# Holding half of the second pass's late weights in a pair of group buffers, with a closer pace for conv backward and parameter chunks

## The chip, the cores and the metric

The kernel runs on one core of one Trainium2 chip. The metric is the device time of one execution in microseconds (us). The core has five engines with a queue each: TensorE (PE, matrix products, with its weight loads listed as PEld), VectorE (DVE), ScalarE (ACT), GpSimd (POOL) and SyncE (SP), and 16 DMA engines, which all queues share. Each engine works through its own instructions in the order fixed when the kernel is compiled; an instruction that waits holds up those behind it.

## The reference

Forward and backward of one block on 2048 tokens of width D = 576: a layer norm, a state-space convolution (S4) with N = 128 states per channel, and a gated feed-forward layer with F = 4608 hidden units.

```
xn = layernorm(x)
s  = conv(xn, K) + xn * Dskip,   K = Re sum_n C exp(dt A l) dt B   (by FFT, length 2 L)
h  = silu(xn @ w1) * (xn @ w3)
g  = silu(h @ w2)
out = x + s * g
return out, and gradients by x, A_re, A_im, B_re, B_im, C_re, C_im, log_dt, Dskip, w1, w3, w2
```

The part that matters here is the gradient by x through the feed-forward layer: with GG and GU the gradients at the two hidden products (2048 x 4608 each), it is GG @ w1^T + GU @ w3^T, added to the gradient from the convolution and taken through the layer norm.

## The kernel before

Tokens are cut into 16 row tiles of 128 (LT), the hidden width into 36 f tiles of 128 (FT) or 18 groups of 256 (FG, NG). A framework places tiles in memory, makes all waits and orders the instructions of each engine by a priority in planned microseconds, which the code sets with `at(us)`; instructions of different parts are so woven into each other. A planned unit takes more than one real microsecond: the backward part starts at unit 700, which is 850 us in the trace, and the second pass at unit 1348, which is 1700 us.

The backward part (L1125) lays these strands beside each other:

- 18 groups, one each 36 units (L1157 to L1161). A group loads its transposed w2 slice (SP) and the stored forward values G and U (POOL) into one of two sets of three buffers, `gg_n`, `h_n` and `gu_n`, 8 KB per partition each. Even groups use the set `e_in0`, odd groups `e_in1` (L1139, L1188). It computes GG and GU in place, stores them to DRAM (L1236), and forms the gradients of w2 (L1251), w3 and w1 (L1270, L1276, L1278). The last even group is 16, the last of all is 17.
- The conv backward (L876) in four quarters of D, `TQ` = 75 units each: transforms on TensorE, complex products on VectorE, copies on ScalarE.
- The parameter chunks (L902): 36 chunks of 16 channels, one each `TC` = 14 units from the end of conv on. Each is loaded two chunks ahead (`gz`, `pz`, and `qT` by a transposing DMA, L1007 to L1012), takes 16 small products (L1025), then 8 products and 4 reduces on VectorE (L1032, L1036). After them comes `phase5_final` (L1040), the gradients of the state-space parameters.
- The second pass (`phase6_inputs`, L1285) from unit T2 = T0 + 36 * 18 = 1348 on: for each row tile it loads GG and GU transposed (`ggc`, `guc`, L1300, 36 f tiles each, in `x_in`, two sets) and multiplies them with the transposed weights (L1312), 144 products per row tile, one row tile each `TX` = 18 units. Then `finish` adds the conv gradient and does the layer norm's backward.

The transposed weights (L1166) are cut by f tiles into parts. Part 0 (f tiles 0 to 15) is in `x_wA` and loaded 150 units before T2. Parts 1 and 2 (16 to 25, 26 to 35) are in `x_wB`, in memory that the groups' buffers free. Each part is 5 transposing DMAs per matrix: four of 128 rows of D and one of 64. The first two row tiles (`head` = 2) are worked part by part, so that products can start before all weights are there; their loads are issued by parts too (L1329 to L1334). Row tile 2 takes the buffers of row tile 0 when that one is done. All transposing DMAs go through SP's queue, mixed with chunk loads and stores of outputs.

The memory of the two stacks is taken in the order in which the pools are opened: on the left `persist`, then `go_keep` (the kept output gradient, 37 KB), then `e_w`, `e_in0`, `e_in1`; when the groups end, `x_in` and `x_wB` take that space from the bottom.

Of the kernel before, what the change touches and what calls it, by code (L numbers as in the profile page):

```python
# [14 lines left out]
BF16 = mybir.dt.bfloat16  # L15
I32 = mybir.dt.int32
P = 128
# [43 lines left out]
class K:  # L61
# [1063 lines left out]
    def backward(self, T0, TG, TQ, TC, TX, gctx, mats):  # L1125
        nc, cfg = self.nc, self.cfg
        D, L, LT, F, FT = cfg.D, cfg.L, cfg.LT, cfg.F, cfg.FT
        self.GG_dram = self.dram.tile([LT, P, F], BF16, name="GG_dram")
        self.GU_dram = self.dram.tile([LT, P, F], BF16, name="GU_dram")
        self.GXN_dram = self.dram.tile([P, LT, D], FP32, name="GXN_dram")  # L1130
        NG = F // self.FG
        T2 = T0 + TG * NG
        FA = 16
        pool = self.tc.tile_pool
        PS = bass.MemoryType.PSUM
        with ExitStack() as out:
            ffn = ExitStack()
            wp = ffn.enter_context(pool(name="e_w", bufs=2))
            inp = [ffn.enter_context(pool(name=f"e_in{k}", bufs=1)) for k in range(2)]  # L1139
            elp = ffn.enter_context(pool(name="e_el", bufs=3))  # L1140
            gwp = ffn.enter_context(pool(name="e_gw", bufs=2))
            ps_h = ffn.enter_context(pool(name="e_ps_h", bufs=3, space=PS))
            ps_gw = ffn.enter_context(pool(name="e_ps_gw", bufs=2, space=PS))
            ps = out.enter_context(pool(name="b_ps", bufs=3, space=PS, side="right"))
            self.ssm_bwd_conv(T0, TQ, ps)
            mats.close()
            fix = out.enter_context(pool(name="b_fix", bufs=1, side="right"))
            S_all = fix.tile([P, 4, D], FP32, name="S_all")
            wA = out.enter_context(pool(name="x_wA", bufs=1, side="right"))
            self.at(T2 - 150)  # L1150
            wT = [self.load_wT(wA, 0, FA)]
            T1 = T0 + 4 * TQ
            self.ssm_bwd_params(T1, TC, S_all, ps)
            self.at(T1 + TC * D // 16)
            self.phase5_final(out, fix, S_all, ps, T1 + TC * D // 16, TX)
            cur = self.phase6_load(0, T0 - TG, TG, wp, inp)
            for gi in range(NG):  # L1157
                nxt = self.phase6_load(gi + 1, T0 + TG * gi, TG, wp, inp) if gi + 1 < NG else None
                self.at(T0 + TG * gi)
                self.phase6_group(gi, cur, elp, gwp, ps_h, ps_gw)  # L1160
                cur = nxt  # L1161
            ffn.close()
            gctx.close()
            self.phase6_inputs(T2, TX, FA, wT)

    def load_wT(self, pool, f0, f1):  # L1166
        cfg = self.cfg
        tiles = []
        for w in ("B_w1", "B_w3"):
            t = pool.tile([P, f1 - f0, cfg.D], BF16, name=f"wT{w}{f0}")  # L1170
            for (do, dsz) in cfg.dch:
                self.nat_transpose(t[:, :, do:do + dsz], self.aps[w][do:do + dsz, f0 * P:f1 * P])
            tiles.append(t)
        return tiles

    def nat_transpose(self, dst, src):
        self.nc.sync.dma_start_transpose(out=dst, in_=src)  # L1177
# [107 lines left out]
    def phase6_inputs(self, T2, TX, FA, wT):  # L1285
        nc, cfg = self.nc, self.cfg
        D, DT, L, LT, F, FT = cfg.D, cfg.DT, cfg.L, cfg.LT, cfg.F, cfg.FT
        aps = self.aps
        pieces = self.dpieces()
        with self.tc.tile_pool(name="x_in", bufs=2) as inp, \  # L1290
                self.tc.tile_pool(name="x_wB", bufs=1) as wB, \
                self.tc.tile_pool(name="l_sb", bufs=2) as sb, self.tc.tile_pool(name="l_sm", bufs=4) as sm, \
                self.tc.tile_pool(name="x_ps", bufs=2, space=bass.MemoryType.PSUM) as ps:
            FM = (FA + FT) // 2
            parts = [(0, FA), (FA, FM), (FM, FT)]
            head = 2

            def load(tiles, i, f0, f1):
                for t, src in zip(tiles, (self.GG_dram, self.GU_dram)):
                    self.nat_transpose(t[:, f0:f1, :], src[i][:, f0 * P:f1 * P])  # L1300

            def alloc(i):
                acts = [inp.tile([P, FT, P], BF16, name=n) for n in ("ggc", "guc")]
                px = [ps.tile([P, 512], FP32, name=f"px{pi_}") for pi_ in range(len(pieces))]
                return acts, px

            def products(acts, px, p):
                f0, f1 = parts[p]
                for fi in range(f0, f1):
                    for ai, act in enumerate(acts):  # L1310
                        for pi_, (po, pw) in enumerate(pieces):
                            nc.tensor.matmul(px[pi_][:, 0:pw], lhsT=act[:, fi, :], rhs=wT[p][ai][:, fi - f0, po:po + pw],  # L1312
                                             start=(fi == 0 and ai == 0), stop=(fi == FT - 1 and ai == 1))

            def finish(i, px):
                gx = sb.tile([P, D], FP32, name="gx7")
                gxs = sb.tile([P, D], FP32, name="gxs7")
                nc.scalar.dma_start(out=gxs[:], in_=self.GXN_dram[:, i, :])
                go_t = sb.tile([P, D], BF16, name="go7")
                nc.scalar.dma_start(out=go_t[:], in_=aps["grad_out"].flatten_outer_dims()[i * P:(i + 1) * P, :])  # L1320
                for pi_, (po, pw) in enumerate(pieces):
                    nc.vector.tensor_tensor(out=gx[:, po:po + pw].rearrange("p (g d) -> p g d", g=4),  # L1322
                                            in0=px[pi_][:, 0:pw].rearrange("p (g d) -> p g d", g=4),
                                            in1=self.perm(gxs[:])[:, :, pi_, :], op=ALU.add)
                self.ln_bwd_tile(sb, sm, gx, i, go_t)

            self.at(T2)
            first = [alloc(i) for i in range(head)]
            for i in range(head):  # L1329
                load(first[i][0], i, *parts[0])  # L1330
            for p in (1, 2):
                wT = wT + [self.load_wT(wB, *parts[p])]
                for i in range(head):
                    load(first[i][0], i, *parts[p])  # L1334
            for p in range(3):
                for i in range(head):
                    self.at(T2 + TX * (head * parts[p][0] + i) / FT)
                    products(*first[i], p)
            for i in range(head):
                finish(i, first[i][1])  # L1340
            for i in range(head, LT):
                self.at(T2 + TX * i)
                acts, px = alloc(i)
                load(acts, i, 0, FT)
                for p in range(3):
                    products(acts, px, p)
                finish(i, px)

# [30 lines left out]
def kernel(  # L1379
# [34 lines left out]
    k = K(tc, aps, {})  # L1414
    with k.ctx:
# [4 lines left out]
        mats = ExitStack()  # L1420
# [3 lines left out]
        with tc.tile_pool(name="xT", bufs=1) as xp, tc.tile_pool(name="kg_sel", bufs=1) as selp:  # L1424
            k.prologue(matp, selp, xp)
            with tc.tile_pool(name="f_w", bufs=2) as wp, \
# [5 lines left out]
                k.ffn_output_open(octx, 345)  # L1432
                k.ffn_hidden(wp, gup, fps, 0, 12)
        k.parp_ctx.close()
        gctx = ExitStack()
        gop = gctx.enter_context(tc.tile_pool(name="go_keep", bufs=1))
        k.go_o = gop.tile([P, k.cfg.LT, k.cfg.D], BF16, name="go_o")
# [1 line left out]
        k.goTt = gop.tile([P, k.cfg.L // 2], BF16, name="goTt")  # L1439
        k.ffn_output(480, 10)  # L1440
        octx.close()
        k.backward(700, 36, 75, 14, 18, gctx, mats)


# [28 lines left out]
```

## Time and profile before

| | |
|---|---|
| median of 7 runs | 2079.49 us (2045.48 to 2086.46) |
| profiled execution: its time, its span | 2084.68 us, 2082.9 us |
| granted TensorE clock, mean | 0.943 |
| PE, DVE, ACT, POOL busy | 86%, 72%, 47%, 22% of the span |
| DMA, mean rate | 202 GB/s |
| second-pass products (L1312) | 2304, 488.2 us busy, 60.8 us idle ahead of them |
| parameter products and reduces (L1032, L1036) | 288 of 683 ns, 144 of 1215 ns |
| chain that ended last: second-pass products | 9.4% of the span |

A row of busy time names the engine, the operation and what is written from what; busy time on PE overlaps itself, since products are pipelined: one of 293 ns follows another of its kind after some 122 ns (142 of them took 17.6 us in the chain of waits). Idle time of an engine counts only where it lies on the path that ends last. The last product of the groups ends at 1700.7 us, the last product of all at 2075.9 us.

### The profile page before, as it was taken

Reading aid. Unit: us, or ns where it says so; the run is one execution under the profiler, and the core shown is the slowest. Engines: PE = TensorE matmul, PEld = TensorE weight load, DVE = VectorE, ACT = ScalarE, POOL = GpSimd, SP = SyncE. Lnnn points to the kernel's source line nnn. Section 1 sums busy time; section 2 is a strip of 40 time slices with the busy share of each in tenths; the row PEclk is TensorE's granted clock in tenths of the full one; section 3 lists DMA queues with packets and bytes.
Section 4 is the critical chain, followed back from the end, with each engine's and each line's share of the span. In section 5 each row is a group of like instructions: output and inputs, shape, how many; then the busy total and the mean of one; then the engine's idle time right before and its main releaser. Section 6 shows DMA issues by size and latency. Waiting matters only on the chain. (4 is left out here: it accounts for less than half of the span.)

```text
span 2082.9 us, 40279 instructions
## 1 busy us (share of the span) xinstructions
PE 1798.8 (86%) x16144; PEld 1251.9 (60%) x16214; DVE 1505.9 (72%) x2616; ACT 971.6 (47%) x1735; POOL 460.8 (22%) x610
## 2 busy tenths in 40 slices
PE   2888988889898899989999999977996994699997
PEld 1443333335453577777777777756685772577785
DVE  7459999998684465477787877775995883586862
ACT  1968888886455411574747465433543410000000
POOL 6015556562122111111111211211121210000000
PEclk9899999999999999999999999988998996799998
DMA  6688778777578887546464645999698799999794
GB/s 180 237 277 284 263 263 280 269 266 259 169 269 186 226 206 183 174 132 190 134 187 137 203 122 149 265 213 196 184 204 178 190 188 191 217 229 176 169 182 63
DMA packets 550380, 421.27 MB, mean 202 GB/s; under 512 B 413872, under 2 KB 480624, under 8 KB 545584
## 3 DMA queue, kind: packets, MB, share of 16 engines
q1 hardware_dynamic: 487648, 254.56, 50.9%
q0 software_dynamic: 37904, 147.48, 22.1%
q10 hardware_dynamic: 24640, 16.65, 3.1%
q8 instruction: 127, 2.08, 0.4%
q14 instruction: 61, 0.50, 0.1%
HBM read 135.96 MB, written 196.27 MB: 159 GB/s over the span
## 5 line engine op out<-in xcount | busy, mean ns | idle before, releaser
L1312 PE MATMUL px<-wTB_w,guc 128*128 128x288 bf16 x1152 | 243.6, 293 | 31.9 <-DMA guc<-GU_dram 21.3
L1312 PE MATMUL px<-wTB_w,ggc 128*128 128x288 bf16 x1152 | 244.6, 293 | 28.9 <-DMA wTB_w<-in_B_w_dram 16.1
L1270 PEld LDWEIGHTS <-xn_bf 128*128 128x128 bf16 x2304 | 224.3, 98 | 29.3 <-issue 2.6
L1032 DVE TENSOR_TENSOR pr_q<-et_ps,pz 128x512 f32<-128x512 f32 x288 | 185.9, 683 | 59.2 <-PE et_ps L1025 52.0
L768 PEld LDWEIGHTS <-xnT 128*128 128x128 bf16 x1152 | 102.8, 99 | 175.6 <-issue 81.6
L1224 PE MATMUL ph<-w2T,goT 128*128 128x256 bf16 x1152 | 180.2, 288 | 2.0 <-DVE e L840 2.0
L1036 DVE TENSOR_REDUCE S_all<-pr_q 128x16 f32<-128x1024 f32 x144 | 174.9, 1215 | 2.3
L1251 PE MATMUL pgw<-go_o,h_n 128*128 128x288 bf16 x1152 | 163.5, 291 | 0.0
L768 PE MATMUL pg<-wmB_w,xnT 128*128 128x512 bf16 x523 | 151.1, 394 | 9.1 <-issue 5.6
L768 PE MATMUL pu<-wmB_w,xnT 128*128 128x512 bf16 x565 | 153.5, 388 | 5.0 <-ACT u_t L778 3.9
L1312 PEld LDWEIGHTS <-guc 128*128 128x128 bf16 x1152 | 114.4, 100 | 65.0 <-DMA guc<-GU_dram 23.4
L1312 PEld LDWEIGHTS <-ggc 128*128 128x128 bf16 x1152 | 114.8, 100 | 60.0 <-issue 14.1
L1358 ACT ACTIVATE t<-gx 128x576 f32<-128x576 f32 x16 | 10.9, 684 | 296.4 <-DVE gx L1322 296.4
L1272 ACT CAST gw<-pgw 128x256 bf16<-128x256 f32 x144 | 54.6, 380 | 196.7 <-PE pgw L1270 195.1
L831 PE MATMUL po<-w2g,hc 128*128 128x288 bf16 x1152 | 145.1, 288 | 1.3 <-ACT u_t L778 1.3
L499 POOL COPY pz_k<-p_k 128x256 bf16<-128x256 bf16 x144 | 132.3, 962 | 47.4 <-issue 38.2
L1270 PE MATMUL pgw<-gu_n,xn_bf 128*128 128x256 bf16 x1152 | 132.8, 272 | 1.5 <-ACT gw L1255 1.1
L1230 DVE TENSOR_TENSOR gu_n<-gh,gu_n 128x1024 bf16<-128x1024 bf16 x72 | 49.4, 686 | 117.1 <-ACT gh L1227 117.1
L831 PEld LDWEIGHTS <-hc 128*128 128x128 bf16 x1152 | 112.1, 98 | 31.2 <-issue 1.7
L1224 PEld LDWEIGHTS <-goT 128*128 128x128 bf16 x1152 | 103.7, 102 | 43.9 <-issue 12.8
L1270 PE MATMUL pgw<-gg_n,xn_bf 128*128 128x256 bf16 x1152 | 129.4, 273 | 0.0
L1251 PEld LDWEIGHTS <-h_n 128*128 128x128 bf16 x1152 | 112.3, 100 | 28.3 <-issue 0.7
(315 smaller groups left out, 3921.0 us busy)
## 6 DMA issues: line engine op xcount, KB each, us to landing
G_dram<-g_t POOLq DMA_DIRECT2D x72, 256.0 KB, 4.0
U_dram<-u_t POOLq DMA_DIRECT2D x72, 256.0 KB, 3.7
H_dram<-h_t SPq DMA_DIRECT2D x72, 256.0 KB, 3.3
Q_dram<-q_k SPq DMA_DIRECT2D x36, 512.0 KB, 4.2
gg_n<-G_dram POOLq DMA_DIRECT2D x18, 1024.0 KB, 5.7
h_n<-U_dram POOLq DMA_DIRECT2D x18, 1024.0 KB, 9.3
GU_dram<-gu_n POOLq DMA_DIRECT2D x36, 512.0 KB, 6.2
GG_dram<-gg_n POOLq DMA_DIRECT2D x36, 512.0 KB, 8.8
```

The costliest lines, as they stand in the source:

```text
L499: nc.gpsimd.tensor_copy(out=pz[:, g, h, 1:3], in_=pv[:, g, h])
L768: nc.tensor.matmul(pt[:], lhsT=xnT[:, c, ts], rhs=wm[w][:, c, :], start=(c == 0 and not first), stop=(c == nfull - 1 and first))
L831: nc.tensor.matmul(po_[:, pi_, 0:pw], lhsT=hc[:, fi, :], rhs=w2[fi][:, po:po + pw], start=(fi == 0), stop=(fi == FT - 1))
L1032: nc.vector.tensor_tensor(out=pr[:, r].rearrange("p k m a -> p m k a"), in0=T[h][:, r][:, None].to_broadcast([P, 2, 4, 2, AV]), in1=pz[:, ...
L1036: nc.vector.tensor_reduce(out=S_all[:, :, d0:d0 + 4].rearrange("p (s k) d -> p k s d", k=2), in_=pr[:].rearrange("p r k (s d) a -> p k s d ...
L1224: nc.tensor.matmul(ph[j][:, k, :], lhsT=lw, rhs=rh, start=(n == 0), stop=(n == nfull))
L1230: nc.vector.tensor_tensor(out=pair(t_)[:, :, sl], in0=gh[:], in1=pair(t_)[:, :, sl], op=ALU.mult)
L1251: nc.tensor.matmul(pgw[pi_][:, 0:pw], lhsT=hn[:, tt, fl * P:(fl + 1) * P], rhs=go_o[:, tt, po:po + pw], start=(tt == 0), stop=(tt == LT - 1))
L1270: nc.tensor.matmul(pw_[:, 0:FG], lhsT=self.xn_bf[:, tt, c * P:(c + 1) * P], rhs=nat[:, tt, :], start=(tt == 0), stop=(tt == LT - 1))
L1272: nc.scalar.copy(out=gw[:, c, :], in_=pw_[:, 0:FG])
L1312: nc.tensor.matmul(px[pi_][:, 0:pw], lhsT=act[:, fi, :], rhs=wT[p][ai][:, fi - f0, po:po + pw], start=(fi == 0 and ai == 0), stop=(fi == F ...
L1358: nc.scalar.activation(out=t[:], in_=g, func=ACT.Copy, scale=-invD, accum_out=mg[:])
```

## The change

Four things are edited. The pool `e_in0` is opened before `go_keep` and stays open to the end, so that its three buffers can be used in the second pass. The f tiles 16 to 35 are cut in three parts instead of two, of 7, 7 and 6 f tiles (NH = 16 * 256 // 576 = 7 is what fits in one buffer): w1 and w3 of the first of them and w1 of the second are put into the three buffers of `e_in0`, with a priority of T2 - 40, ahead of the last group; w3 of the second and both of the third go to `x_wB`, which is smaller by that. The first two row tiles are allocated and loaded with priority T2 - 15 instead of T2, in four parts. And TQ goes from 75 to 65, TC from 14 to 13, so that conv ends at unit 960 instead of 1000 and the chunks at 1428 instead of 1504.

```diff
-            inp = [ffn.enter_context(pool(name=f"e_in{k}", bufs=1)) for k in range(2)]
+            inp = [self.in0, ffn.enter_context(pool(name="e_in1", bufs=1))]
...
     def load_wT(self, pool, f0, f1):
         cfg = self.cfg
-        tiles = []
-        for w in ("B_w1", "B_w3"):
-            t = pool.tile([P, f1 - f0, cfg.D], BF16, name=f"wT{w}{f0}")
-            for (do, dsz) in cfg.dch:
-                self.nat_transpose(t[:, :, do:do + dsz], self.aps[w][do:do + dsz, f0 * P:f1 * P])
-            tiles.append(t)
-        return tiles
+        return [self.load_wT1(pool.tile([P, f1 - f0, cfg.D], BF16, name=f"wT{k}_{f0}"), k, f0, f1) for k in range(2)]
+
+    def load_wT1(self, t, k, f0, f1):
+        for (do, dsz) in self.cfg.dch:
+            self.nat_transpose(t[:, :, do:do + dsz], self.aps[("B_w1", "B_w3")[k]][do:do + dsz, f0 * P:f1 * P])
+        return t
...
-            FM = (FA + FT) // 2
-            parts = [(0, FA), (FA, FM), (FM, FT)]
+            NH = LT * self.FG // D
+            parts = [(0, FA), (FA, FA + NH), (FA + NH, FA + 2 * NH), (FA + 2 * NH, FT)]
+            held = lambda name: self.in0.tile([P, LT, self.FG], BF16, name=name)[:].rearrange(
+                "p t f -> p (t f)")[:, 0:NH * D].rearrange("p (f d) -> p f d", d=D)
...
-            self.at(T2)
+            self.at(T2 - 40)
+            wT = wT + [[self.load_wT1(held(n), k, *parts[1]) for k, n in enumerate(("gg_n", "h_n"))]]
+            wT = wT + [[self.load_wT1(held("gu_n"), 0, *parts[2])]]
+            self.at(T2 - 15)
             first = [alloc(i) for i in range(head)]
-            for i in range(head):
-                load(first[i][0], i, *parts[0])
-            for p in (1, 2):
-                wT = wT + [self.load_wT(wB, *parts[p])]
+            for p in range(len(parts)):
+                if p == 2:
+                    wT[2].append(self.load_wT1(wB.tile([P, NH, D], BF16, name="wTB2"), 1, *parts[2]))
+                if p == 3:
+                    wT = wT + [self.load_wT(wB, *parts[3])]
                 for i in range(head):
                     load(first[i][0], i, *parts[p])
-            for p in range(3):
+            for p in range(len(parts)):
                 for i in range(head):
                     self.at(T2 + TX * (head * parts[p][0] + i) / FT)
                     products(*first[i], p)
...
-                for p in range(3):
+                for p in range(len(parts)):
                     products(acts, px, p)
...
         k.parp_ctx.close()
+        k.in0 = k.ctx.enter_context(tc.tile_pool(name="e_in0", bufs=1))
         gctx = ExitStack()
...
-        k.backward(700, 36, 75, 14, 18, gctx, mats)
+        k.backward(700, 36, 65, 13, 18, gctx, mats)
```

## The prediction

> **What bounds the kernel now.** I read the slices of the page first, then the busy time by stage, then what TensorE waited for in the last stage, then the transfer queue of SP in the gap that this showed.
>
> ```profile
> PE   2888988889898899989999999977996994699997
> DMA  6688778777578887546464645999698799999794
> ```
> Each digit is a slice of 52 us. TensorE is nearly full except at slices 30 and 33 to 34, where the transfers stand at 9 tenths. The stages say it in microseconds (columns: stretch, length, busy time and count of PE, weight loads, DVE, ACT, POOL, then granted clock, transfer share, GB/s):
>
> ```profile
> 850.00:1310.00 460.00, 427.35 (x4376) 348.03 (x4374) 344.43 (x667) 287.62 (x675) 77.12 (x111) 0.98 0.54 163
> 1310.00:1700.00 390.00, 333.08 (x3014) 260.16 (x3013) 300.38 (x408) 157.25 (x262) 76.84 (x105) 0.91 0.91 201
> 1700.00:1800.00 100.00, 50.55 (x399) 37.58 (x396) 56.32 (x76) 1.92 (x5) 1.54 (x3) 0.74 1.08 215
> 1800.00:2040.00 240.00, 233.49 (x1930) 183.89 (x1927) 160.88 (x434) 12.04 (x29) 0.00 (x0) 0.98 0.91 180
> ```
> The first row is conv backward beside groups 0 to 8, the second the parameter chunks beside groups 9 to 17. The last group ends at 1700.7; the second pass then needs 96 us until it runs at its full rate at 1797. What TensorE waited for from 1700 on (total, times, longest):
>
> ```profile
> PE px L1312 <- DMA wTB_w<-in_B_w_dram: 24.6, 4, 14.0
> PE px L1312 <- DMA guc<-GU_dram: 21.3, 7, 6.2
> PE px L1312 <- DMA ggc<-GG_dram: 12.8, 2, 11.5
> ```
> The SP queue in that gap (start, length, what):
>
> ```profile
> 1720.39 2.93 SPq L1177 DMA_TRANSPOSE wTB_w<-in_B_w_dram  x2
> ...
> 1730.53 5.76 SPq L1177 DMA_TRANSPOSE wTB_w<-in_B_w_dram  x4
> ...
> 1736.97 24.19 SPq L1177 DMA_TRANSPOSE wTB_w<-in_B_w_dram  x14
> 1761.21 1.72 SPq L1177 DMA_TRANSPOSE guc<-GU_dram  x1
> ```
> So 20 weight transposes hold SP for 32.9 us (2.93 + 5.76 + 24.19), and three loads for row tiles 0 and 1 come only behind them. Then row tile 2 waits: its first load is issued at 1781.1 behind three chunk loads (1766.5 to 1781.0), and TensorE idles 11.5 and 5.5 us until 1797.
>
> **What the skill says.** The Trainium skill, "DMA: Bandwidth & Descriptors", section "Issuing engines are not separate DMA queues": transfers started by different engines share the same 16 DMA engines. The trace agrees: share 1.08 in the gap with SP alone issuing most of it. So moving a transfer earlier pays only as far as there is room earlier. The same page, "Latency and other measured facts", gives 261 GB/s for transposing DMAs; here the run of 14 (2 of 64 rows in each 10, so 295 KB on average, 4.1 MB) took 24.2 us, 171 GB/s, and I use the trace. "Perfetto Trace Analysis", section "Optimization Strategy": where the most contended engine changes over time, interleaving regimes can help. The trace has such regimes: row two has DVE at 77%, the rows after it have few vector operations but transfers and TensorE.
>
> **The change, part by part.**
>
> 1. *Weights held in the last even group's buffers.* Of f tiles 16 to 35 of two matrices (40 tile columns, 147 KB each, 5.9 MB), 21 go into the three buffers of e_in0 (7 each; 3.1 MB in 15 transposes), 19 stay behind the last group (2.8 MB, 15 smaller transposes). Group 16's last matmuls end at 1663.8 and its stores were issued by 1651.8, so the buffers are free near 1664 (their landing, 9 us in the median, fits). The 15 remaining transposes cost SP between 15.6 us (32.9 x 19/40, by bytes) and 24.6 (15 x 1.64, by count); the shortest one in the trace, 1.28, gives 19.2. I take 20: 13 us leave the gap. The moved 15 cost as much, 20 us by count and 18 by bytes at 171 GB/s, between 1664 and 1700. The transfers stood there at
>
> ```profile
> 1664.00:1684.00 20.00, 19.72 (x181) 14.46 (x180) 19.31 (x27) 5.83 (x13) 3.19 (x5) 1.00 0.72 125
> 1684.00:1701.00 17.00, 16.84 (x172) 14.65 (x172) 12.35 (x15) 3.41 (x11) 4.12 (x6) 1.00 1.10 225
> ```
> so 28% of 20 us, 5.6 us, is free for certain; but 125 GB/s beside 225 shows that the first stretch wasn't at its rate, and at 225 it would have room for 9 us. The rest pushes on the loads of heads (row tiles 0 and 1, part 0), which landed at 1702, and on two chunk loads queued in the same SP order. Cost at the start of the pass: 3 to 11 us, I take 5.
>
> 2. *Four parts, heads loaded at T2 - 15 instead of T2.* The loads of heads become 16 pieces instead of 12; four more at the 1.3 us floor of such a piece is 5 us of SP. They have the go_keep space in both versions and wait for the last gradient of w2 (1684). Being 15 units earlier can't get them past that wait: nothing. TensorE no longer stands on part 1: its 28 f-tile products of two heads, 56 matmuls at 122 ns, 7 us, run while the rest of the weights land. Of the 24.6 us of weight waits I count 20 gone (13 us of SP and 7 of cover), and the 5 us of pieces against it.
>
> 3. *Row tile 2.* It takes the buffer of row tile 0, and can be loaded only when that one's last part is done. Now that is the last 6 f tiles instead of 10, so TensorE has 2.9 us of row tile 1 left as cover instead of 4.9: 2 us lost. The 6.2 us wait on guc behind the weights goes, since loads of heads no longer stand behind all of them; of the three chunk loads ahead of row tile 2 (15 us) I count one gone, 5 us. Gain 6 + 5 - 2 = 9 us. The gap in sum: 20 - 5 - 5 + 9 = 19 us shorter.
>
> 4. *Conv backward 75 to 65, chunks 14 to 13.* Nothing is removed: per chunk 8 vector products (683 ns) and 4 reduces (1215 ns), 10.0 us of DVE when overlap is taken off (185.9 + 174.9 over 36). Conv now spans 260 units, 7.2 groups instead of 8.3 (9 ran in fact). A group costs TensorE 34 us and DVE 10.9 (16 operations at 0.68). So row one: PE 427 - 1.8 x 34 = 366, DVE 344 - 20 = 324, ACT stays near 250; with its 33 us of idle and some more for the ACT copies of gk_st (17.4 us of PE wait today) 405 us. Row two: 10.8 groups and 29 chunks (388/13) instead of 9 and 23: PE 333 + 61 + 6 = 400, DVE 300 + 20 + 60 = 380, up to 418 (10.8 x 10.9 + 30 x 10) if I build it up instead. Today's idle of PE is 57 us, most of it ACT blocked behind the load of gg_n (54.2 us, 6 times) with PE queued behind a parameter product (38.4 us on pr_q). Keep that: 455 us. End of the last group: 850 + 405 + 455 = 1710, 10 us later than now.
>
> 5. *Later.* 6 chunks less stand in the pass: 6 us of PE and 33 us of transfers (0.9 MB each at 170), and phase5_final ends before the last row tiles. PE waits after 1800 on guc and ggc are about 9 us, and the last row tile lost 12 us at 2041 to 2056 behind a 14.9 us ggc transpose. I take 13 us in all, the 6 of TensorE and a third of these 21; bounds 6 and 27.
>
> 6. *e_in0 opened earlier.* 24 KB stay reserved through the output stage. That space was freed by the forward pools before either of its users starts; no instruction is added. Nothing; a bad overlap would show as a wait of go_o near 700, a few us.
>
> Sum: -19 - 13 + 10 = -22 us on the profiled execution's own 2084.7 us, that is 2063. Its time is 5 us over the median of 2079.5, so I state 2057.
>
> **Rivals.**
>
> - *All waits go and DVE never decides* (2030): the pass starts without the 24.6 us, the later gain is at its bound of 27 us, the last group ends at 1700. For it: DVE has 90 us idle in row two. Against: transfers at 1.1 there. 19 + 5 (what is left of the weight waits) + 27 = 51 us; 2079 - 51 = 2028, stated as 2030.
> - *The transfers are only shifted* (2077): 18 us of transposes into 5.6 us of free room push the loads of heads by 12, so 7 more than I took, the gap shrinks by 12, and row tile 2 gets nothing of its 9: 3 us; parts 4 and 5 nearly cancel (10 against 13, less what the later tail doesn't give). For it: share 0.91 over row two; within 0.5% of before.
> - *DVE becomes the bound of the chunk stage* (2100). In-order TensorE stands behind a parameter product that waits for pr_q, with the group's matmuls queued behind it. DVE needs up to 418 us there; if it keeps 80 of the 90 us idle that load waits give it today, the stage is 498, the last group ends at 1753, 53 late, against 32 won: 21 slower. It decides from 59 us of idle on (418 + 59 = 477, 32 late). For it: the waits on loads that make this idle (gg_n, qT 12.2 us) get no shorter with denser chunk loads. Against: DVE was at 25 of 25 us in stretches of conv without TensorE dropping.
>
> **How the numbers follow.** Forecast 0.40, all waits go 0.18, only shifted 0.13, DVE the bound 0.29. Faster 0.58, same 0.13, slower 0.29; 0.5% (10 us) is what a measurement can tell from no change. The seven runs of before spread over 41 us by themselves (2045 to 2086), more than my steps; the range takes that in below: 2012 (all waits go, and a median that falls among the short runs) to 2094. The forecast's own range is 2040 to 2070.
>
> **What would show it.** Steps 1 to 3: transposes of weights between 1664 and 1700, waits of px on weights under 8 us, the gap from the last pgw to row tile 2 near 77 us instead of 96. Step 4: last pgw at 1710, DVE share of the stage near 85 to 90%, waits on pr_q no more than 60 us. Step 5: no qT transfer once row tile 6 is loaded. I am wrong if the last group ends after 1735, or if the head loads land 12 us later and take the place of the weight waits.

## The result and the profile after

The kernel after takes 2096.11 us in the median of 27 runs, the kernel before on the same chip 2085.42 us in the median of 64: by the medians it is 0.5% slower. The ratio is 1.010, with a 95% interval of 1.0067 to 1.0132; it, like every ratio below, compares fast runs alone, those within 1.5% of the fastest run of their kernel, and so depends on single short runs and can differ by as much as a per cent from that of the medians. So the change makes the kernel 0.5 to 1% slower. Forecast was 22 us less. Single times of one kernel scatter over some 30 to 80 us (before: 2045 to 2120), so every comparison of times below rests on several runs where it can; what is read from a profile is read from one execution. The profiled execution of after took 2088.27 us (span 2086.5, granted clock 0.948), 8 us under its own median, and is only 3.6 us longer than the profiled one of before (2084.68). The trace therefore shows a mild case of the loss.

The slices of the page of after, TensorE and the transfers:

```profile
PE   2888989889898999988888888697999995699988
DMA  6678788777579996545454457998888799988974
```

A slice is 52 us. The two low slices, 34 and 35, are still there; where before had a row of 9 in slices 18 to 25 there are more slices of 8. By stage the windows view says it in microseconds (stretch, length, busy time and count of PE, weight loads, DVE, ACT and POOL, then granted clock, transfer share, GB/s). The limits are the first load of a parameter chunk, the end of the last group and the end of the span:

```profile
850.00:1292.00 442.00, 393.77 (x4016) 320.36 (x4015) 329.94 (x637) 265.41 (x634) 67.58 (x96) 0.97 0.52 150
1292.00:1719.00 427.00, 371.75 (x3385) 290.46 (x3384) 356.76 (x484) 175.21 (x289) 85.63 (x117) 0.93 0.94 213
1719.00:2086.00 367.00, 305.09 (x2462) 239.19 (x2456) 179.29 (x467) 15.31 (x38) 1.16 (x3) 0.91 0.84 165
```

Length less the first number is idle time of TensorE: 48, 55 and 62 us. In before the same three stages are 460, 391 and 382 us with 33, 57 and 69 us idle. So conv ends 18 us sooner, the last group ends 18.6 us later (its last product starts at 1719.2 against 1700.6), and the second pass is 15 us shorter. In the first two stages together TensorE is busy 4 us longer (more chunks fall into them) and idle 14 us longer; the 14 are nearly all in the conv stage.

What TensorE waited for from 1700 on in after (total, times, longest):

```profile
PE et_ps L1025 <- DMA qT<-Q_dram: 26.7, 1, 26.7
PE px L1313 <- DMA ggc<-GG_dram: 15.6, 3, 6.3
PE px L1313 <- DMA guc<-GU_dram: 11.9, 3, 5.3
```

The waits on weights, 24.6 us in before, are gone. One wait of 26.7 us has come in their place, and it belongs to another part of the kernel: a parameter product (`et_ps`) waits for its chunk's `qT`. The timeline of TensorE around it (start, length, what, in brackets the idle time before it and its releaser):

```profile
1754.67 0.29 PE L1313 MATMUL px<-h_n,guc 128*128 128x288 bf16 x1
1781.64 0.61 PE L1025 MATMUL et_ps<-gz,qT 128*128 128x128 bf16 x4 [26.68 <-DMA qT<-Q_dram]
1782.04 0.45 PE L1313 MATMUL px<-h_n,guc 128*128 128x288 bf16 x1
```

The second-pass products on both sides use the held weights (`h_n`), which were all issued by 1714. They stood still because a parameter product was ahead of them in TensorE's order. The SP queue of after shows why its operand was late:

```profile
1665.15 16.55 SPq L1176 DMA_TRANSPOSE h_n<-in_B_w_dram  x5
...
1688.53 4.57 SPq L1176 DMA_TRANSPOSE gg_n<-in_B_w_dram  x3
...
1693.78 2.66 SPq L1176 DMA_TRANSPOSE gg_n<-in_B_w_dram  x2
1696.67 1.24 SPq L1176 DMA_TRANSPOSE gu_n<-in_B_w_dram  x1
...
1701.81 12.53 SPq L1176 DMA_TRANSPOSE gu_n<-in_B_w_dram  x4
...
1720.81 2.81 SPq L1176 DMA_TRANSPOSE ggc<-GG_dram  x1
...
1746.64 7.05 SPq L1176 DMA_TRANSPOSE wTB<-in_B_w_dram  x5
...
1756.55 13.46 SPq L1176 DMA_TRANSPOSE wT<-in_B_w_dram  x10
...
1776.65 2.76 SPq L1176 DMA_TRANSPOSE qT<-Q_dram  x1
```

Three things are to be seen. The 15 held transposes occupy SP for 16.55 + 4.57 + 2.66 + 1.24 + 12.53 = 37.6 us. The first load of a head row tile (`ggc`) comes at 1720.8, 1.6 us after the last group's end; in before it comes 17 us ahead of that end. And the `qT` that TensorE needs stands behind the last heads and the 15 remaining weight transposes (7.05 + 13.46 = 20.5 us). In before the heads' first load, and the two `qT` loads around its 14 weight transposes, were:

```profile
1683.76 6.30 SPq L1177 DMA_TRANSPOSE ggc<-GG_dram  x1
...
1724.65 5.84 SPq L1177 DMA_TRANSPOSE qT<-Q_dram  x1
...
1767.68 2.60 SPq L1177 DMA_TRANSPOSE qT<-Q_dram  x1
```

So before, too, has a stretch of 43 us in which no `qT` load is issued (1724.65 to 1767.68), as long as that of after (1734.38 to 1776.65). TensorE didn't run into it there, since it stood waiting for weights first.

During the wait the transfers were not at their fullest:

```profile
1755.00:1782.00 27.00, 0.36 (x4) 0.36 (x5) 6.09 (x7) 0.00 (x0) 0.00 (x0) 0.56 0.83 167
```

Their share is 0.83, where the 27 us before (1719 to 1746) have 1.04, while SP issues piece after piece with hardly a pause from 1746.64 on, most of them 1.2 to 1.4 us apart. So at this point the number of pieces on SP's queue may count for more than their bytes; no run separates the two.

### The profile page after: what moved, and what is told of

Same layout as the page of the kernel before. It is cut to its first block, busy times and chain, and to the rows that moved or that the text cites. A ratio compares the mean times of both kernels' runs of the same rounds, so it can differ in the third digit from the quotient of the medians.

```text
span 2086.5 us, 40311 instructions
## 1 busy us (share of the span) xinstructions
PE 1800.7 (86%) x16144; PEld 1254.9 (60%) x16214; DVE 1505.6 (72%) x2616; ACT 970.0 (46%) x1733; POOL 462.6 (22%) x610
## 5 line engine op out<-in xcount | busy, mean ns | idle before, releaser
L1313 PE MATMUL px<-wT,ggc 128*128 128x288 bf16 x704 | 149.3, 294 | 15.6 <-DMA ggc<-GG_dram 15.6
L1313 PE MATMUL px<-wT,guc 128*128 128x288 bf16 x704 | 148.7, 294 | 11.9 <-DMA guc<-GU_dram 11.9
L499 POOL COPY pz_k<-p_k 128x256 bf16<-128x256 bf16 x144 | 134.2, 975 | 48.2 <-issue 38.7
L1250 PEld LDWEIGHTS <-h_n 128*128 128x128 bf16 x1152 | 113.5, 101 | 32.9 <-issue 2.5
L1025 PE MATMUL et_ps<-gz,qT 128*128 128x128 bf16 x576 | 55.9, 227 | 75.9 <-DVE pr_q L1032 38.2
```

The source lines that it names most:

```text
L499: nc.gpsimd.tensor_copy(out=pz[:, g, h, 1:3], in_=pv[:, g, h])
L1025: nc.tensor.matmul(T[h][:, :, dd].rearrange("p r k (f t) -> p r (k f) t", f=2), lhsT=qT[:, dl, :], rhs=gK[:, :, :, :, dl, :].rearrange("p ...
L1250: nc.tensor.matmul(pgw[pi_][:, 0:pw], lhsT=hn[:, tt, fl * P:(fl + 1) * P], rhs=go_o[:, tt, po:po + pw], start=(tt == 0), stop=(tt == LT - 1))
```

## The experiments

The first theory was that the two halves of the change, held weights and closer pace, have separate effects, the weights a small gain that is eaten by the new wait, the pace a loss. Its rivals: the weights cost by what they push into a full stage, or the pace loses only together with them. All ratios are to before, measured on the same chip; "median" is that of the kernel's own runs, beside which before's own was 2084.42 to 2086.07 us.

**The halves.** Held weights alone, all of the change but the pace:

```diff
-        k.backward(700, 36, 65, 13, 18, gctx, mats)
+        k.backward(700, 36, 75, 14, 18, gctx, mats)
```

> The changed kernel with the old pace of 75 and 14: the held weights alone. Theory A (the closer pace costs the time): the last group ends near 1701 us as before, and with the gap of 91 us that the changed kernel has (96 before) the time is 0 to 8 us under before. Theory B (the held weights stand in SP's queue ahead of the head loads and of qT): the gap stays at 90 us or grows, with head loads issued only after the held weights, and the time is 5 to 20 us over before. On a wait of TensorE for qT of over 15 us in the gap B counts, on none A.

Measured: 0.9919 (0.9872 to 0.9965), median 2073.48 us of 22 runs. The time is that of theory A, a little better; the wait on `qT`, 25.7 us in its profile, is the sign named for theory B. So the wait is there without a loss beside before. Its SP queue, the held transposes and the first head:

```profile
1639.30 8.28 SPq L1176 DMA_TRANSPOSE h_n<-in_B_w_dram  x3
...
1650.22 2.60 SPq L1176 DMA_TRANSPOSE gg_n<-in_B_w_dram  x2
...
1658.36 3.94 SPq L1176 DMA_TRANSPOSE gg_n<-in_B_w_dram  x3
1662.48 2.57 SPq L1176 DMA_TRANSPOSE gu_n<-in_B_w_dram  x2
...
1665.73 4.37 SPq L1176 DMA_TRANSPOSE gu_n<-in_B_w_dram  x3
...
1680.10 4.16 SPq L1176 DMA_TRANSPOSE ggc<-GG_dram  x1
```

The pace alone, on the kernel before:

```diff
-        k.backward(700, 36, 75, 14, 18, gctx, mats)
+        k.backward(700, 36, 65, 13, 18, gctx, mats)
```

> The kernel before with pace 65 and 13: the closer pace alone. Theory A: the last group ends 15 to 20 us later than before (1716 to 1721), the second pass is shorter by 5 to 10, the time 8 to 15 us over before. Theory B: the last group ends within 8 us of before and the time is at or under before by up to 10 us.

Measured: 1.014 (1.0109 to 1.0171), median 2098.72 us of 22 runs (0.7% by the medians). The two have opposite signs, and the product of the ratios, 1.006, is near the 1.010 of the whole (their intervals overlap). So the loss is the pace's. Its windows, cut at the same events:

```profile
850.00:1287.00 437.00, 388.31 (x4006) 318.59 (x4005) 330.15 (x637) 263.44 (x630) 66.70 (x96) 0.98 0.52 152
1287.00:1726.00 439.00, 373.64 (x3389) 291.28 (x3386) 357.08 (x484) 174.97 (x289) 85.41 (x117) 0.93 0.91 204
1726.00:2096.00 370.00, 303.45 (x2454) 236.99 (x2452) 179.30 (x467) 15.31 (x38) 1.09 (x2) 0.92 0.86 167
```

They repeat those of after: 49 us idle in the conv stage, and a second pass of 370 us instead of 382 without any held weights. Of the 15 us by which after's second pass is shorter, 12 are so the pace's (fewer chunks left over) and 3 the weights'. The heads start 13 us ahead of the last group's end:

```profile
1712.89 6.47 SPq L1177 DMA_TRANSPOSE ggc<-GG_dram  x1
```

That is 4 us less than in before. The other 14 of the 18 us by which they come late in after (1.6 us behind the end) are there only with the held weights.

**The pace taken apart.** Conv alone (`65, 14` on before):

```diff
-        k.backward(700, 36, 75, 14, 18, gctx, mats)
+        k.backward(700, 36, 65, 14, 18, gctx, mats)
```

> The kernel before with conv backward at 65 and the chunks left at 14: chunks start 40 units earlier and end 40 earlier. Theory A with its cost in the crowding of conv: the stage from 850 us to the start of the chunks shrinks by less than it should and the time is 5 to 12 us over before. If the cost is in the density of the chunks, this one is within 5 us of before.

Chunks alone (`75, 13` on before):

```diff
-        k.backward(700, 36, 75, 14, 18, gctx, mats)
+        k.backward(700, 36, 75, 13, 18, gctx, mats)
```

> The kernel before with conv at 75 and the chunks at 13. Theory A with its cost in the density of the chunks (DVE and transfers per group): the last group ends 8 to 20 us later and the time is 5 to 12 us over before. If the cost is in conv, this one is within 5 us of before.

Measured: 1.0018 (0.9975 to 1.0061), median 2088.9 us of 14 runs, and 0.9987 (0.9957 to 1.0018), median 2076.85 us of 22. Each alone changes nothing that can be told, yet together they cost 1.4%, so neither the crowding of conv nor the density of the chunks is the cost by itself. The profiles show one thing clearly: at conv pace 65 TensorE idles 48.2, 48.7 and 47.8 us in the conv stage (after, pace alone, conv alone), at 75 it idles 31 to 36 us in six kernels (before 32.6). The waits of TensorE from 850 to 1310 say where, before:

```profile
PE et_ps L606 <- ACT gk_st L979: 17.4, 18, 3.1
PE ph L1224 <- ACT gh L1227: 6.2, 6, 1.6
...
PE et_ps L606 <- DVE gx L1000: 1.3, 1, 1.3
```

and after:

```profile
PE et_ps L606 <- ACT gk_st L979: 17.1, 19, 3.1
PE ph L1223 <- ACT gh L1226: 13.4, 8, 3.9
PE et_ps L606 <- DVE gx L1000: 5.2, 1, 5.2
```

The wait on ACT's conv copies doesn't grow. What grows is the wait of the groups' first products (`ph`) on ACT's step for a group (`gh`), and one wait of conv on DVE: 7.2 and 3.9 us of the 15. Conv ends only 11 to 23 us sooner for that (first chunk load at 1287 to 1299 against 1310), and 8 groups instead of 9 are done by then. But conv alone has this idle time too, at a ratio of 1.0018, so it can't by itself be the 1.4%.

Two more points of the pace, closer conv (`55, 14`) and closer chunks (`65, 12`), both on before:

```diff
-        k.backward(700, 36, 75, 14, 18, gctx, mats)
+        k.backward(700, 36, 55, 14, 18, gctx, mats)
```

> The kernel before with conv at 55 and chunks at 14, the suspected cost doubled. If conv backward is bound by its own chain on DVE and ACT, the first qT comes hardly earlier than with 65 (1285 to 1295 us), TensorE's idle time up to it is 58 to 70 us, and the time is 8 to 20 us over before. If conv follows its pace, the first qT comes near 1270 and the idle time stays near 48.

```diff
-        k.backward(700, 36, 75, 14, 18, gctx, mats)
+        k.backward(700, 36, 65, 12, 18, gctx, mats)
```

> The kernel before with conv at 65 and chunks at 12, to double the second half of the pace. 65 with 14 was 0.2% over before, 65 with 13 1.4%. If the density of the chunks behind an early conv is the cost, 2 to 3% over before, with TensorE idle 70 to 85 us in the chunk stage (47 at 14, 65 at 13). If those 65 us were chance of one order, it is between 0 and 1.4% over and the idle time of that stage is 45 to 65 us.

Measured: 1.0201 (1.0122 to 1.028), median 2113.49 us, and 1.0155 (1.0065 to 1.0245), median 2115.7 us, 6 runs each. With conv at 55 the first chunk load comes at 1254.6, so conv does follow the pace, and its stage idles 45 us, no more than at 65: conv is not held back by a chain of its own. With chunks at 12 the ratio is the same as at 13 within the intervals, and less than the 2 to 3% expected of chunk density; the chunk stage idles 54.6 us, as in after (55.2), and the conv stage 46.9. By the medians chunks at 14, 13 and 12 behind conv at 65 take 2088.9, 2098.7 and 2115.7 us, so that a cost of their density behind an early conv is not excluded. The idle time there doesn't grow with DVE's load: at a DVE share of 84% (after, 356.8 of 427 us), 81% (pace alone, 65.4 us idle) and 79% (conv at 55, 60.0 us idle) it is what five kernels of 75, 14 show with DVE at 75 to 79% (44 to 71 us, before 56.9).

The other way, conv farther paced (`85, 14` on before):

```diff
-        k.backward(700, 36, 75, 14, 18, gctx, mats)
+        k.backward(700, 36, 85, 14, 18, gctx, mats)
```

> The kernel before with conv at 85 and chunks at 14, no held weights. If the loose conv alone gives what the held weights with 85 gave, 0.8% or more under before. If the two are needed together or the held weights carry it, within 0.4% of before.

Measured: 0.9891 (0.9849 to 0.9932), median 2062.97 us of 20 runs. A slower conv makes the kernel faster. The gain isn't in the conv stage: TensorE idles 42 us there, with one group more in it, against 33 in before. Its chunk stage and its second pass:

```profile
1358.00:1667.00 309.00, 287.30 (x2668) 226.49 (x2669) 261.73 (x356) 135.92 (x229) 66.61 (x92) 0.98 0.88 224
...
1667.00:2048.00 381.00, 311.99 (x2592) 244.90 (x2588) 252.78 (x562) 15.62 (x38) 1.28 (x3) 0.91 0.94 187
```

The chunk stage idles 22 us instead of 57, and the second pass is as long as before (382) although it has more chunks in it. What ACT waits for between 1250 and 1740 shows the difference: the load of a group's `gg_n` in before

```profile
ACT L1197 <- DMA gg_n<-G_dram: 55.0, 7, 17.8
```

and with conv at 85

```profile
ACT L1197 <- DMA gg_n<-G_dram: 20.0, 7, 6.8
```

With 10 groups done by the first chunk load instead of 9, fewer groups have to fetch their inputs beside the chunks' loads. That fits, but is not tested by itself: this wait is 30 to 55 us in the five kernels of 75, 14, so before is at the top of them, and 38.2 us in after, which has more groups beside chunks than before (9.5 against 8.5).

**The gap.** Is the new wait on `qT` an accident of order that can be mended by itself? On the held weights alone, the last two parts of the heads and the late weights were given priorities 4 and 8 units after T2 instead of 15 before it, so that chunk loads come between them:

```diff
             for p in range(len(parts)):
+                self.at(T2 + (-15, -15, 4, 8)[p])
                 if p == 2:
```

> Held weights at the old pace, with the loads of parts 2 and 3 (heads and weights) at T2 + 4 and T2 + 8 instead of T2 - 15, so that two chunk loads go between them on SP. If the 25.7 us that TensorE waited for qT is the price of the order on SP, the wait falls under 8 us, some of it comes back as a wait of px for weights (5 to 10 us), and the time is 8 to 15 us under the held weights alone, 1.2 to 1.6% under before. If the transfers as such are the bound of the gap, the wait only changes its name and the time stays within 5 us of the held weights alone.

The waits of TensorE in the second pass, held weights alone:

```profile
PE et_ps L1025 <- DMA qT<-Q_dram: 25.7, 1, 25.7
PE px L1313 <- DMA guc<-GU_dram: 19.6, 6, 7.8
PE px L1313 <- DMA ggc<-GG_dram: 11.0, 2, 6.4
```

and with the chunk loads between:

```profile
PE px L1313 <- DMA ggc<-GG_dram: 27.7, 3, 11.9
PE px L1313 <- DMA guc<-GU_dram: 23.5, 9, 5.5
...
PE et_ps L1025 <- DMA qT<-Q_dram: 1.2, 1, 1.2
```

The wait on `qT` fell from 25.7 to 1.2 us, those on `ggc` and `guc` rose from 30.6 to 51.2: 56.3 us before the edit, 52.4 after it. The wait changed its name, and the second pass went from 380 to 378 us. Its ratio of 0.9873 (0.9815 to 0.9931) is not to be told from that of the held weights, as its 22 runs spread from 2034 to 2114 us around a median of 2085.12, near that of before (2086.07). So the gap is bound by what must pass through the queue and the transfers in it, and the order only chooses who stands at the end. The opposite test takes the transfers away. This kernel leaves the 20 late weight transposes of before out, and multiplies f tiles 16 to 35 with part 0's weights, so its gradient by x is another quantity:

```diff
-                wT = wT + [self.load_wT(wB, *parts[p])]
+                wT = wT + [[t[:, 0:parts[p][1] - parts[p][0], :] for t in wT[0]]]
```

> The kernel before without the 20 late weight transposes: the products of f tiles 16 to 35 read the weights of part 0 instead, so the gradient by x is not the reference's; everything else is done. It prices the weights in the gap, and is the most that holding all of them could give. If the weights are the bound of the gap: the 24.6 us wait goes, SP loses 33 us, the first load of row tile 2 goes out near 1750 instead of 1781, and the time is 25 to 33 us under before (1.2 to 1.6%). If loads of ggc, guc and chunks bound it next: the gap shrinks by 10 to 18 us only, waits on ggc and guc rise over 45 us, the time is 8 to 18 us under before.

Measured: 0.9873 (0.9786 to 0.996), median 2043.78 us of 6 runs: 26 us under before by the ratio, 42 by the medians, where 25 to 33 were expected if the weights bound the gap. The second pass of before and of this kernel:

```profile
1701.00:2083.00 382.00, 313.29 (x2532) 243.24 (x2529) 225.01 (x526) 15.43 (x38) 1.10 (x2) 0.90 0.90 177
```

```profile
1700.00:2041.00 341.00, 306.72 (x2532) 239.93 (x2529) 224.99 (x526) 15.45 (x38) 1.09 (x2) 0.96 0.94 177
```

The same work of TensorE, 41 us shorter, with its idle time down from 69 to 34 us. The other 7 us are busy time: the same 2532 products take 306.72 instead of 313.29 us, at a mean granted clock of 0.96 instead of 0.90. From the last group's end to row tile 2 at full rate it takes 56 us instead of 96. So 20 transposes in the gap are worth 40 us of one profiled execution, 2 us each, and taking half of their bytes out could, by estimate, have been worth some 20 (half of 40), or 15 after the 5 us of SP that the forecast gave the smaller head pieces. Held, they brought 10.6 us of gap (96.4 to 85.8, held weights alone), of which 8.3 were lost again behind row tile 2, and 3.1 us with the close pace (94.4 to 91.3).

**Where the held weights alone gain.** Their profile puts only 2 us into the second pass; the last group ends 14 us sooner. Does the early place of `e_in0` alone do that? It was opened early in before, and closed with the groups:

```diff
-            inp = [ffn.enter_context(pool(name=f"e_in{k}", bufs=1)) for k in range(2)]
+            inp = [self.in0, ffn.enter_context(pool(name="e_in1", bufs=1))]
...
+            self.in0ctx.close()
...
+        k.in0ctx = ExitStack()
+        k.in0 = k.in0ctx.enter_context(tc.tile_pool(name="e_in0", bufs=1))
```

> The kernel before with only the pool e_in0 opened ahead of go_keep (and closed with the groups, so that no weight is held): other addresses, nothing else. The held-weights kernel of the old pace was 0.8% faster, but its profile shows the second pass as long as before (380 us from the last group to the end, 382 before) and the last group 14 us earlier. Theory place: the earlier last group comes from where and when e_in0 is laid, and this kernel gives at least half of the 0.8% (8 us). Theory held: the gain belongs to the moved weights, and this kernel is within 0.3% of before.

Measured: 1.0105 (1.0019 to 1.019), median 2096.18 us of 6 runs (0.5% over before's). It is no gain, so the place is not the source of the 0.8%. The end of the last group in kernels of pace 75, 14 scatters between 1687 and 1706 in single profiles, so 14 us there prove nothing. What the 0.8% are was not found.

**Both together.** Held weights with conv at 85, and at 95:

```diff
-        k.backward(700, 36, 65, 13, 18, gctx, mats)
+        k.backward(700, 36, 85, 14, 18, gctx, mats)
```

> Held weights with conv backward looser, 85 and 14. TensorE's idle time from 850 us to the first qT was 33 to 36 us in three kernels with 75 and 48 to 49 in three with 65. If a closer conv costs TensorE by standing behind DVE and ACT, 85 takes 5 to 12 us more off that idle time, while the chunks start later and 3 more are left for the second pass: a time within 8 us of the held weights alone. If 75 is already loose, the idle time stays above 30 and the time is 5 to 10 us over the held weights alone.

```diff
-        k.backward(700, 36, 65, 13, 18, gctx, mats)
+        k.backward(700, 36, 95, 14, 18, gctx, mats)
```

> Held weights with conv at 95 and chunks at 14. If looser is better, 1.3% or more under before, near or under the one with 85. If 85 is at the foot, it lies 0.3 to 1% over that one, since 3 more chunks (1.1 us of TensorE and 5 us of transfers each) come into the second pass.

Measured: 0.9867 (0.9773 to 0.996), median 2047.44 us of 6 runs, and 0.9957 (0.9908 to 1.0007), median 2082.1 us of 22 runs. The first beats both kernels of this study and has the lowest median of those that do all the work; whether it beats conv at 85 without held weights (0.9891) the intervals don't say, and its one profiled execution (2072.03 us) was the longest of its six. At 95 more chunks are left: by the last group's end 20 are issued instead of 25 with the held weights at 75, and the second pass takes 408 us instead of 380. With conv at 85 less idle time in the conv stage was expected, 5 to 12 us; it was 41.7 us instead of 33.7, so the gain is not the one that was looked for. By conv pace, 55, 65, 75 and 85 without held weights, the medians are 2113, 2089, 2085 and 2063 us; with them, 75, 85 and 95, they are 2073, 2047 and 2082. Of the paces tried 85 is the best, in the direction opposite to the change.

## Why the prediction was wrong

In the terms of its sum, on the profiled executions: the gap from the last group's end to row tile 2 at full rate was to shrink by 19 us and shrank by 5 (96.4 to 91.3); the last group was to end 10 us later and ended 18.6 later; the rest was to gain 13 and gained 10. That is -5.1 + 18.6 - 9.9 = +3.6 us where the forecast had -22. The medians differ by 11 us, as the profiled execution of after was a quick one.

The waits of TensorE inside the gap, before and after, give the 5 us term by term. At the start of the pass it waits 1.0 and 8.0 us for the heads' loads, so 7 us are lost where step 1 had 5. Weights take 24.6 us and none, `qT` none and 26.7, so step 2 loses 2 us where it was to gain 15. The later waits on `guc` take 7.0 us and none, those at row tile 2 16.9 and 9.3, so step 3 gains 14.6 us where it had 9. The term that failed is that of step 2.

- *Step 1, cost of the moved transposes: mis-sized on SP, near as a wait.* Forecast 20 us of SP and a push of 3 to 11 us on the heads' loads. Held weights alone came close: 8.28 + 2.60 + 3.94 + 2.57 + 4.37 = 21.8 us, and heads that begin 6.6 us ahead of the last group's end instead of 17, 10 us later. Together with the pace the same 15 took 37.6 us, and the heads came 18.4 us later against the group's end, 4 of them by the pace alone. The named sign of failure, heads 12 us late, came true; as a wait of TensorE the push measured 7 us, within the range.
- *Step 2, "of the 24.6 us of weight waits I count 20 gone": this is the step that failed.* They went, all of them, but the step took a wait away without asking which operand would be next to be late in the whole of TensorE's order. It asked only about row tile 2. The parameter products are woven in between, and the loads for them stand behind the last head pieces and 15 weight transposes on SP: 26.7 us. The stretch of 43 us without a `qT` load was to be read in the trace of before. The experiments with the chunk loads between and without the late transposes show that this wait is only the form, and what must pass in the gap the substance. On the amount the forecast's own arithmetic held (20.5 us of SP for weights in the gap, forecast 32.9 - 13 = 19.9), but it counted those 13 us of SP as time of TensorE.
- *Step 3, row tile 2: right, and by more than forecast.* Its two waits before full rate were 4.39 and 4.95 us instead of 11.5 and 5.5, and the wait on `guc` behind the weights went. The way was another: of the chunk loads ahead of its first load none was gone, four stood there (1775.5 to 1794.6) instead of three, but that load (1796.25) then waited for row tile 0's buffer and not for them. The time in front of it was already lost.
- *Step 4, the pace: wrong in one term.* TensorE's work came out right (row one 394 against 366 for 7.2 groups; 8 ran, and 0.8 of a group at 34 us is the 28), and so did DVE (357 against 380), the waits on `pr_q` (37.9 us, forecast no more than 60) and the idle time of the chunk stage (55, forecast 455 - 400). The idle time of the conv stage, "33 us of idle and some more", was taken as 39 and is 48: 9 us, which in the sum is the whole difference between +10 and +18.6. It is there in all four kernels with conv at 65 (46.9 to 48.7 us), also in conv alone, which isn't slower; so the sum of this one execution closes with it, but the loss over many runs is not explained by it.
- *Step 5, later: right.* 9.9 us against 13; the last `qT` is issued at 1808.9 instead of 1883.4.
- *Step 6, `e_in0` early: nothing forecast.* No wait shows in the chunk or conv stages, but alone it measured 1.0105 (1.0019 to 1.019) in 6 runs, 0.5% by the medians; whether it costs anything stays open.

Of the rivals, "DVE becomes the bound" named 2100 us, close to the measured time by luck, for a reason that the runs do not support: the last group ended at 1719 and not at 1753, and TensorE's idle time in the chunk stage did not rise with DVE's share. "Only shifted" came near on the gap (3 us forecast, 5 measured), but by luck: it counted a further delay of the heads and no gain at row tile 2, not the wait on `qT`; and it let the pace's loss and its later gain cancel. What no case had is the extra idle time in the conv stage, and the wait of a parameter product in the gap.

Open: why conv at 65 and chunks at 13 cost nothing measurable each and 1.4% together; where the held weights' 0.8% arise; whether bytes or places on SP bound the gap; and whether the 22 us idle of the chunk stage at conv 85 is typical, since the combination with held weights has the lower median with 54 us idle in its profile, and that with 95 has 18 us and isn't faster.

## What to carry to other kernels

When a wait is removed, walk the in-order queue of the waiting engine to the next operand that is not there yet, over all strands woven into that queue, and count what must still pass through the issuing queue before it: if that is much the same, expect the wait to come back under another name. A strand paced ahead of its place does no less work, and here closer conv and chunks together gained nothing; so try the pace in both directions before trusting the one that looks natural. Measure the parts of a bundled change alone, since here a gain of 0.8% and a loss of 1.4% came as one change.

## What the runs showed of the hardware

The time that a transposing DMA holds SP's queue depends on what else is moving: 15 transposes of the same sizes took 21.8 us in the kernel with held weights alone and 37.6 us in after. Where the transfer share was 0.83 to 0.97 in these two profiles, each held SP for about 1.3 us; where it was 1.03 to 1.19, for 1.2 to 3.3 us. The share alone doesn't settle it: five of them took 16.55 us at a share of 1.19, and five of the same sizes 7.05 us at 1.11. Size made no difference at the low end: in the run of ten at 1756.55 the two pieces of 64 rows took 1.26 us each, those of 128 rows 1.23 to 1.29. The Trainium skill, "DMA: Bandwidth & Descriptors", section "Issuing engines are not separate DMA queues", says that transfers started by different engines share the same DMA engines; that the held transposes took longer at shares of 1.03 to 1.19 agrees with it.

TensorE's granted clock was lower where it stood still: 0.56 in after's wait for `qT` (1755 to 1782) and 0.60 in before from 1720 to 1737 (1.37 us busy of 17), against 1.00 in before from 1701 to 1720 (17.26 us busy of 19). With fewer waits the same products took less time, as the 7 us of the kernel without the late transposes show.

Executions of one kernel on this single core spread over 3.6% (before: 2045 to 2120 us), and two of after's 27 times were 4184 and 8133 us; a profile of one execution can therefore lie on the wrong side of a difference of 1%. The spread goes with the mean granted clock (two runs of before: 0.939 at 2134.24 us, 0.958 at 2054.55); which of the two follows the other, and how much of the differences between kernels has to do with it, no run here shows.
